# Units 2 to 5 of a gated linear attention: inputs as runs of tokens, transposed by VectorE, with level decays and row products on GpSimd

## The chip, the cores and the metric

The kernel runs on one core of a Trainium2 chip. The metric is device time in microseconds: how long one execution takes, as the median of several.

## The reference

Two blocks follow each other. The first is a gated linear attention over 4 batches, 8 heads, 768 tokens and head size 48. The second is a mixture of four experts whose input is the first one's output, 3072 tokens by 384.

```python
for t in range(S):
    state = alpha[:, :, t, :, None] * state + np.einsum('bhd,bhe->bhde', k[:, :, t], v[:, :, t])
    y[:, :, t] = np.einsum('bhd,bhde->bhe', q[:, :, t], state)
...
p = domain_probs / (domain_probs.sum(-1, keepdims=True) + 1e-09)
for e in range(E):
    h = np.maximum(x @ w1[e], 0.0)
    out += p[:, e:e + 1] * (h @ w2[e])
```

`w1` is 384 x 1024 and `w2` 1024 x 384 for each expert. All inputs and outputs are float32.

## The kernel before

**Units and groups.** A unit is a block of 128 tokens of one batch, all heads: 24 units, numbered in the order in which they are done. Groups of units go through the experts together: units 0 and 1 (group 0), then four groups of four, then units 22 and 23. For each group and expert there is an `up` (eight chunks of 128 hidden columns: `x @ w1` into a PSUM tile `one`, ReLU by ScalarE) and a `down` (`h @ w2` into `ops`, which VectorE adds to the output with the probabilities as a scale, L1079).

**Precision.** Group 0 multiplies plain float32. From group 1 on the weights and activations are split into a high and a low part, and three products are made (`PRODUCTS`, L103; the products with the low part of the activations come last in `down`). VectorE makes the low part of the hidden values in `hidden_rest` (L1009), ahead of `down`. The weights are read from the inputs once, as float32 pieces (`raw`, `load_piece`, L234 for `w1` and L238 for `w2`, four pieces of 384 KB for each matrix and expert), split by ScalarE and VectorE (`split_piece`, L252 and L254), stored to device memory from GpSimd's queue (L255), and read back as pairs later (L225).

**Attention is woven in.** While the experts work on one group, the attention of the next group's units is made beside it. Each unit is a Python generator with about 15 to 20 steps. `deal` (L1099) gives each step a due time from estimated costs, and `advance` (L1155), which is called between expert matmuls, runs the steps that are due. So each engine's queue has a fixed order in which expert and attention instructions alternate, and a waiting instruction holds up everything behind it on its engine. The start is ordered by hand (L1184 to L1196).

**A unit's steps.** Inputs `a` (the decay), `k`, `q` come with tokens in the partitions and have to be transposed to have channels in them (`AT`, `KT`, `QT`; `QT` is multiplied by `AT`). Then come seven levels, each of twice the block size. At a level `li`, ScalarE copies half of QT to a buffer (`copy_q`, L777 or L543), VectorE multiplies half of QT by the decays (`next_q`, L784 or L549) and then multiplies pairs of decays in place to get those of the next level (L786 or L551), and `next_k` does the same for KT (L795 and L796; L560 and L563). TensorE makes scores from these (`sc`, `far`), VectorE merges them by masks into `near` (L813, L616), ScalarE copies them to `lat`, and TensorE multiplies by the values (`yps`) and makes the state's update (`sps`). The diagonal of the scores, a product of q and k summed over channels (`dot`), is made apart.

**Three ways to take the inputs.** `in_runs` (L144) and `in_fours` (L145) say from which unit on a way is used; they are 6 and 10.

- Units 0 to 5: `load` issues one DMA for each of a, k, q (L176; 192 KB, with 192 bytes in a row), and four TensorE transposes each (`turned`, L285) turn them by way of PSUM. ScalarE copies the results to AT (L728) and KT (L737), and VectorE multiplies the third by AT (L756).
- Units 6 to 9: `load` issues four DMAs for each of a, k, q, whose rows are runs of tokens (L171, into `sa`, `sk`, `sq`), and one DMA each for k and q in the old form (L176, into `rk` and `ra`), for `dot`. VectorE transposes blocks of 32 x 32 (`turn`, L723), ScalarE scales AT (L734), VectorE multiplies QT by AT (L754). When the first such unit is loaded, GpSimd clears the run tails once (L165).
- Units 10 to 23 (`in_order`): as before, but q and the decays for `dot` come in rows of four tokens. GpSimd multiplies decays of neighbouring tokens (L510) and q by them (L512); VectorE multiplies the result by k (L522) and sums it (L523), each in two halves.

For units 1 to 9 `own_terms` (L741) makes `dot`: VectorE multiplies q and k (L743), sums the product (L744), and the next unit's k is asked for. This happens in the unit's second step, for unit 1 in its third.

**Queues.** SyncE issues all loads. Its order around the start is: units 0 and 1, four pieces of `w1` of the first expert, unit 2's a, k, q (from `first_unit`), the probabilities (L1189, 48 KB), four pieces of `w2` (at the first `up`, L238), four pieces of `w1` of the second expert, then unit 2's values. `norm_probs` (L267) turns the probabilities by four TensorE transposes (L270) and norms them on VectorE (L272 to L275). Its place is after the first three products of the first `down`. `fill` (L1184) issues matmuls on zeros at the start.

Of the kernel before, what the change touches and what calls it, by code (L numbers as in the profile page):

```python
# [16 lines left out]
AX = mybir.AxisListType  # L17
# [3 lines left out]
def kernel(  # L21
# [11 lines left out]
    nc = tc.nc  # L33

    B, H, S, D = q.shape
    E, DM, F = moe_w1.shape
    P = 128
# [13 lines left out]
    FOUR = 4  # L51
# [3 lines left out]
    n = np.arange(QUAD)[None, :]  # L55
# [4 lines left out]
    t = np.arange(HALF)[None, :]  # L60
# [30 lines left out]
    half = B // 2  # L91
# [13 lines left out]
    row_k = const.tile([P, H, D], F32, name="rk")  # L105
    row_a = const.tile([P, H, FOUR - 1, D], F32, name="ra")
# [34 lines left out]
    HEAD_FIRST = [*(0.06 * j for j in range(1, 8)), 0.5, 0.58, 0.66, 0.74, 0.82, 0.93]  # L141
    HEAD_SECOND = [0.02, 0.06, 0.1, 0.13, 0.16, 0.2, 0.25, 0.31, 0.37, 0.45, 0.52, 0.61, 0.66]
    REST = [0.05, 0.17, 0.3, 0.42, 0.58]
    in_runs = half + B  # L144
    in_fours = half + 2 * B  # L145
    MARGIN = 6.0
    waiting = deque()
# [140 lines left out]
    def first_unit(fill, other):  # L288
# [139 lines left out]
            nc.scalar.copy(out=later_half[:HALF, NP * i:NP * (i + 1)], in_=far[rows[i]])  # L428
        for i in range(1, NQ):
            load_piece(0, i, behind=later_half[:HALF, 0, :1])  # L430
        load(2, "akq")
        take(2, part(second, 0))
        take(3, part(second, QUAD))
        take(-1, part(second, HALF, HALF))
# [55 lines left out]
    def in_order(u):  # L490
        cb, b = units[u]
        k = u - in_fours
# [16 lines left out]
        for j in range(1, FOUR - 1):  # L509
            nc.gpsimd.tensor_mul(row_a[:, :, j], row_a[:, :, j - 1], row_a[:, :, j])  # L510
        for i, t in enumerate(fours[u]):
            nc.gpsimd.tensor_mul(t[:, :, 1:], t[:, :, 1:], row_a[:, H // 2 * i:H // 2 * (i + 1)])  # L512
        yield
        load(u + 1, "a")
        KT = work.tile([P, NP, P], F32, name="KT", bufs=6)
# [3 lines left out]
        dots = hid.tile([P, H, FOUR], F32, name="dot", bufs=1)  # L519
        for i, t in enumerate(fours.pop(u)):  # L520
            some = slice(H // 2 * i, H // 2 * (i + 1))
            nc.vector.tensor_mul(t, t, row_k[:, some].unsqueeze(2).broadcast_to([P, H // 2, FOUR, D]))  # L522
            nc.vector.reduce_sum(out=dots[:, some], in_=t, axis=AX.X)  # L523
            yield
        load(u + 1, "k")
# [19 lines left out]
        def next_q(li):  # L545
            m = LEVELS[li]
            qv = halves(QT, m)[:, :, :, 1, :]
            dv = halved(decs[li])
            nc.vector.tensor_mul(qv, qv, spread(dv[:, :, :, 0], m))  # L549
            dec = dv[:, :, :, 0] if li < 6 else work.tile([P, NP, 1], F32, name="dec6", bufs=9)  # L550
            nc.vector.tensor_mul(dec, dv[:, :, :, 0], dv[:, :, :, 1])  # L551
            decs.append(dec)

        def next_k(li):
# [156 lines left out]
    def attention(u):  # L711
# [26 lines left out]
        dots = hid.tile([P, H, FOUR], F32, name="dot", bufs=1)  # L738
        dot = dots.rearrange("p h f -> p (h f)")[:, :H]

        def own_terms():  # L741
            own = rk[:, :, :D]
            nc.vector.tensor_mul(own, rq[:, :, :D], rk[:, :, :D])  # L743
            nc.vector.reduce_sum(out=dot, in_=own, axis=AX.X)  # L744
            load(after, "k")


        own_late = u == 1
        if not own_late:
            own_terms()  # L750
        yield
        if u >= in_runs:
            turn("q", QT)
# [1 line left out]
        else:  # L755
            nc.vector.tensor_mul(QT, turned(pair(rq)), AT)  # L756
        if own_late:
            own_terms()
        load(after, "q")
        yield  # L760

# [18 lines left out]
        def next_q(li):  # L780
            m = LEVELS[li]
            qv = halves(QT, m)[:, :, :, 1, :]
            dv = halved(decs[li])
            nc.vector.tensor_mul(qv, qv, spread(dv[:, :, :, 0], m))  # L784
            dec = dv[:, :, :, 0] if li < 6 else work.tile([P, NP, 1], F32, name="dec6", bufs=9)
            nc.vector.tensor_mul(dec, dv[:, :, :, 0], dv[:, :, :, 1])  # L786
            decs.append(dec)

        def next_k(li):
# [159 lines left out]
    def up(gi, e, fc, spent, slots=None):  # L949
        n = len(groups[gi]) * P  # L950
        lo, hi = (slots.start * P, slots.stop * P) if slots else (0, n)
        begins, ends = lo == 0, hi == n
        c, f = divmod(fc, FPQ)
        i = first_piece(gi, e) + c
        if fc == 0 and begins:
            for k in range(NQ):
                hidden[k] = hid.tile([P, 2, FPQ, NT], F32 if gi == 0 else F32R, name="hT", bufs=NQ)
        if gi == fc == 0 and begins:
            for k in range(NQ):
                load_piece(1, e * NQ + k, beside=True)  # L960
        beside = BESIDE[(gi, e) == (1, 0)]
        if fresh(gi) and fc in beside:
            making.append(split_piece(1, first_piece(gi, e) + beside[fc]))
        if gi == 0 and e > 0 and fc in SPLIT_AT:
            making.append(split_piece(0, e * NQ + SPLIT_AT[fc]))
        if gi == 0 and begins and e + 1 < E and fc == (FCH - 1 if e == 0 else FCH // 2):
            for k in range(NQ):
                load_piece(0, (e + 1) * NQ + k)
        col = slice(f * P, (f + 1) * P)
        if gi > 0:  # L970
            w = wt[0][i].rearrange("p t (c f) -> p t c f", f=QF)[:, :, :, col]
        else:
            w = wt[0][i].rearrange("p (c f) -> p c f", f=QF)[:, :, col]
        parts = [hidden[c][:, part, f, lo:hi] for part in range(2)]
        one = ps.tile([P, NT], F32, name="one", tag="g", bufs=4)[:, :hi - lo]
        if gi == 0:
            for kc in range(KC):
                nc.tensor.matmul(one, lhsT=w[:, kc], rhs=xTs[gi][:, 0, kc, lo:hi],  # L978
                                 start=(kc == 0), stop=(kc == KC - 1))
            advance(spent)  # L980
            nc.scalar.activation(out=parts[0], in_=one, func=ACT.Relu)
        else:
            turns = [(kc, *parts) for parts in PRODUCTS for kc in range(KC)]
            for k, (kc, of_w, of_x) in enumerate(turns):
                nc.tensor.matmul(one, lhsT=w[:, of_w, kc], rhs=x_part(gi, of_x)[:, kc, :n],  # L985
                                 start=k == 0, stop=k == len(turns) - 1)
            nc.scalar.activation(out=parts[0], in_=one, func=ACT.Relu)  # L987
            while finish:
                hidden_rest(*finish.popleft())
            finish.append((one, parts))  # L990
        while finish and fc == FCH - 1:
            hidden_rest(*finish.popleft())
        background()
        if f == FPQ - 1 and ends:
            if gi == 0:
                if e == E - 1:
                    load_piece(1, i + NQ, held=wt[1][i])
            elif gi != LAST - 1:
                load_piece(0, i + AHEAD, held=wt[0].pop(i))
            while late:  # L1000
                load_piece(1, late.popleft())
            while stores:
                stores.popleft()()
        if gi > 0:
            advance(spent)
# [155 lines left out]
    with tc.manual_schedule():  # L1161
        nc.scalar.dma_start(out=ident_all, in_=nc.inline_tensor(ident_np, name="ident_c").ap())
        nc.scalar.dma_start(out=masks_all, in_=nc.inline_tensor(mask_np, name="masks_c").ap())
        nc.gpsimd.memset(sts[B - 1], 0.0)
        for nm in "akq":
            for r in (early[nm], apart[nm]):
                nc.gpsimd.memset(r[:, :, D:], 0.0)
        nc.gpsimd.memset(lat[HALF:, :, :HALF], 0.0)
        for t in values + blocks:
            nc.gpsimd.memset(t, 0.0)  # L1170
        for t in sts[:-1]:
            nc.gpsimd.memset(t, 0.0)

        load(0, "aqkv")
        load(1, "akqv")

        idle = ps.tile([P, DM], F32, name="idle", tag="g", bufs=4)
        zeros = sts[B - 1].rearrange("p a i d -> p (a i d)")  # L1180

        def fill(times, n=P):
            for _ in range(times):
                nc.tensor.matmul(idle[:, :n], lhsT=zeros[:, :P], rhs=zeros[:, :n], start=True, stop=True)  # L1184

        runs = [None, attention(1)]
        fill(7)
        runs[0] = first_unit(fill, runs[1])
        nc.sync.dma_start(out=p_rows, in_=moe_domain_probs.rearrange("(n p) e -> n p e", p=P))  # L1189

        span = cost(0, 0, 0) * FCH / 2 + cost(1, 0, 0)
        runs.append(norm_probs())
        waiting.extend((span * (k + 1) / 15, u, runs[u]) for k, u in (
            *((k, 1) for k in range(3)), (3, 0), (4, 1), *((k, 1) for k in range(6, 10)),
            (9.5, 2), (10, 1), (10.5, 0), *((k, 1) for k in range(11, 14))))
        for fc in range(FCH):  # L1196
            up(0, 0, fc, cost(0, 0, 0) / 2, slice(0, 1))
        down(0, 0, [0])
        while waiting:
            next(waiting.popleft()[2], None)  # L1200
        clock = 0.0
        waiting.extend((1.0 + k, 1, runs[1]) for k in range(2))
        waiting.extend(deal())

        for gi, e in tasks:
            rest = gi == e == 0
            for fc in range(FCH):
                up(gi, e, fc, cost(0, gi, e) / (2 if rest else 1), slice(1, len(groups[0])) if rest else None)
            each = len(groups[gi]) if gi > 0 else 1
            turns = [range(k, k + each) for k in range(rest, len(groups[gi]), each)]  # L1210
            for slots in turns:
                down(gi, e, slots)
        while stores:
            stores.popleft()()
# [28 lines left out]
```

## Time and profile before

| what | before |
|---|---|
| median of the runs shown | 972.08 us (971.99 to 972.23, 3 runs) |
| the profiled execution's own time | 971.34 us |
| its span, first to last instruction | 969.3 us |
| mean granted TensorE clock | 1.000 |
| data moved by DMAs | 185.26 MB, 191 GB/s over the span |
| VectorE transpose of 128x512 (L723) | 1.08 to 1.18 us, x12 |
| TensorE transposes (L285) | 116 matmuls of 0.27 us, overlapping |
| ScalarE copies of a transposed input (L728, L737) | 0.58 and 0.59 us, x5 each |
| VectorE decays (L786, L551) | 0.13 to 1.3 us, 158 in all, 48 us |
| VectorE row products (L522) and sums (L523) | 0.95 us each, x28 each |
| GpSimd products of rows (L510, L512) | 1.02 and 1.48 us on average, x28 each |

The profile comes from one execution. In its lists PE is TensorE's matmuls, PEld its weight loads, DVE VectorE, ACT ScalarE, POOL GpSimd and SP SyncE; a q behind the name means the engine's sequencer or DMA queue. A timeline row has a start, a duration, the engine, the line, and what is written from what; in brackets is how long the engine sat idle before it and what ended that. In the chain of work that ended last, a row has a start and the time that its part of the chain took. A row of waits has the total, the number and the longest one.

### The profile page before, as it was taken

The page shows a single profiled execution, that of the slowest core. Times are in us where ns is not written, and L with a number is a line of the kernel's source. Part 1 is how long each engine was busy: PE and PEld are TensorE (multiplying, and loading weights), DVE is VectorE, ACT ScalarE, POOL GpSimd, SP SyncE. Part 2 cuts the span into 40 slices and gives each one's busy share as a digit, 9 for nine tenths or more (in the row PEclk, how much of TensorE's full clock was granted, in tenths as well). Part 3 has the DMA queues.
Part 4 walks back from the last instruction along what each step waited for, and adds up shares of the span by engine and source line. Part 5 has one row for each costly group of instructions (what it writes and reads, how often), then busy time and mean ns, then how long its engine had stood idle before and what let it go on. Part 6 is the DMA issues. An engine that isn't in the chain of part 4 may idle for free.

```text
span 969.3 us, 20948 instructions
## 1 busy us (share of the span) xinstructions
PE 957.8 (99%) x8456; PEld 857.2 (88%) x8456; DVE 585.0 (60%) x1164; ACT 384.4 (40%) x838; POOL 126.6 (13%) x173
## 2 busy tenths in 40 slices
PE   8999999999999999999999999999999999999998
PEld 7787778988979989989889899899898899999997
DVE  6677778477787856757747668668776212221222
ACT  5787656454462441441441432434344122021111
POOL 3000110011213212021121120220220000000000
PEclk9999999999999999999999999999999999999999
DMA  8998859395964787865677864679870007060601
GB/s 164 298 292 247 253 143 325 104 358 143 307 217 129 224 288 208 269 202 136 199 252 204 303 217 113 198 211 253 273 233 16 34 1 260 1 260 2 257 20 33
DMA packets 168740, 185.26 MB, mean 191 GB/s; under 512 B 83980, under 2 KB 148364, under 8 KB 168644
## 3 DMA queue, kind: packets, MB, share of 16 engines
q1 hardware_dynamic: 162180, 154.07, 52.7%
q0 software_dynamic: 6016, 29.49, 8.2%
q8 instruction: 67, 1.10, 0.5%
q10 hardware_dynamic: 448, 0.36, 0.1%
q14 instruction: 29, 0.24, 0.1%
HBM read 151.37 MB, written 32.51 MB: 190 GB/s over the span
## 4 chain that ended last, share of the span: by engine, by line
PE 90%; DVE 5%; ACT 3%; issue 1%; DMA 0%; SPq 0%; DVEq 0%; POOL 0%; ACTq 0%; POOLq 0%
PE ops L1053 41%; PE one L985 33%; PE one L978 4%; PE sc L596 3%; PE yps L670 2%; PE sc L803 2%; PE yps L898 1%; PE tp L285 1%; DVE hT L1009 1%; DVE w L254 1%; ACT qb L777 1%; DVE near L813 1%; PE sps L606 0%; PE far L859 0%; PE idle L1184 0%
## 5 line engine op out<-in xcount | busy, mean ns | idle before, releaser
L1053 PE MATMUL ops<-w,hT 128*128 128x384 f32 x2112 | 377.2, 337 | 2.2 <-DVE hT L1009 2.0
L1053 PEld LDWEIGHTS ops<-w,hT 128*128 128x128 f32 x2112 | 365.3, 188 | 7.9 <-DVE hT L1009 3.9
L985 PE MATMUL one<-xT,w 128*128 128x512 f32 x1440 | 333.2, 391 | 0.1
L985 PEld LDWEIGHTS one<-xT,w 128*128 128x128 f32 x1440 | 269.4, 188 | 56.8 <-DVE hT L1009 1.0
L987 ACT ACTIVATE hT<-one 128x512 fp32r<-128x512 f32 (+1 forms) x192 | 108.0, 562 | 315.5 <-PE one L985 314.9
L1009 DVE SCALAR_TENSOR_TENSOR hT<-one,hT 128x512 fp32r<-128x512 f32 (+1 forms) x192 | 121.1, 642 | 103.6 <-ACT hT L987 103.5
L1079 DVE SCALAR_TENSOR_TENSOR acc<-ops,p_all,acc 128x384 f32<-128x384 f32 x66 | 38.8, 611 | 81.9 <-PE ops L1053 81.8
L549 DVE TENSOR_TENSOR QT<-QT,AT 128x256 f32<-128x256 f32 x70 | 32.9, 471 | 49.6 <-ACT qb L543 39.2
L777 ACT COPY qb<-QT 64x256 f32<-64x256 f32 x126 | 51.5, 409 | 21.3 <-DVE QT L784 13.9
L466 POOL TENSOR_TENSOR st<-st,dec 64x192 f32<-64x192 f32 x32 | 18.6, 582 | 277.9 <-PE yps L670 218.5
L978 PE MATMUL one<-xT,raw 128*128 128x256 f32 (+1 forms) x240 | 45.8, 340 | 0.6 <-issue 0.5
L1053 PE MATMUL ops<-raw,hT 128*128 128x384 f32 x128 | 45.4, 493 | 0.7 <-DMA raw<-in_moe_w_dram 0.7
L1088 POOL DMA_DIRECT2D out_dram<-acc x22 | 12.0, 548 | 249.1 <-DVE acc L1079 249.1
L978 PEld LDWEIGHTS one<-xT,raw 128*128 128x128 f32 x240 | 38.1, 191 | 5.4 <-issue 0.6
L510 POOL TENSOR_TENSOR ra<-ra 128x384 f32<-128x384 f32 x28 | 28.5, 1018 | 99.0 <-DMA ra<-in_alpha_dram 97.4
L255 POOL DMA_DIRECT2D kept<-w x32 | 17.5, 547 | 182.9 <-DVE w L254 83.0
L512 POOL TENSOR_TENSOR raw<-raw,ra 128x576 f32<-128x576 f32 x28 | 40.8, 1478 | 1.1
L784 DVE TENSOR_TENSOR QT<-QT,AT 128x256 f32<-128x256 f32 x60 | 26.0, 434 | 23.6 <-ACT qb L777 23.0
L813 DVE COPY_PREDICATED near<-masks,sc 128x256 f32<-128x256 uint8 x54 | 28.8, 534 | 11.8 <-PE sc L803 10.8
L985 PE MATMUL one<-raw,w 128*128 128x256 f32 x288 | 35.2, 283 | 0.0
L543 ACT COPY qb<-QT 64x256 f32<-64x256 f32 x80 | 32.1, 401 | 7.5 <-DVE QT L549 4.0
L985 PEld LDWEIGHTS one<-raw,w 128*128 128x128 f32 x288 | 35.1, 192 | 0.0
(166 smaller groups left out, 960.8 us busy)
## 6 DMA issues: line engine op xcount, KB each, us to landing
w<-kept SPq DMA_DIRECT2D x108, 768.0 KB, 6.6
kept<-w POOLq DMA_DIRECT2D x32, 768.0 KB, 6.0
raw<-in_moe_w_dram SPq DMA_DIRECT2D x44, 384.0 KB, 7.4
raw<-in_q_dram SPq DMA_DIRECT2D x112, 96.0 KB, 3.0
rv<-in_v_dram SPq DMA_DIRECT2D x24, 192.0 KB, 3.3
out_dram<-acc POOLq DMA_DIRECT2D x22, 192.0 KB, 2.5
rk<-in_k_dram SPq DMA_DIRECT2D x18, 192.0 KB, 3.1
sa<-in_alpha_dram SPq DMA_DIRECT2D x36, 88.0 KB, 3.7
```

The lines of the kernel that those rows point to most:

```text
L512: nc.gpsimd.tensor_mul(t[:, :, 1:], t[:, :, 1:], row_a[:, H // 2 * i:H // 2 * (i + 1)])
L543: nc.scalar.copy(out=qbs[li][rows, :, i, :].rearrange("p a (b r) -> p a b r", r=m), in_=qv[rows])
L549: nc.vector.tensor_mul(qv, qv, spread(dv[:, :, :, 0], m))
L596: nc.tensor.matmul(banks[li // 2 - 1][HALF * s:HALF * (s + 1), li % 2, 2 * p:2 * p + 2, :], lhsT=KTs[li][:, p, HALF * s:HALF * (s + 1)], r ...
L777: nc.scalar.copy(out=qb[rows, :, i, :].rearrange("p a (b r) -> p a b r", r=m), in_=qv[rows])
L813: nc.vector.copy_predicated(near.rearrange("p a (b two r) -> p a b two r", two=2, r=m)[:, :, :, 1, :], mk.unsqueeze(1).broadcast_to([P, H, ...
L978: nc.tensor.matmul(one, lhsT=w[:, kc], rhs=xTs[gi][:, 0, kc, lo:hi], start=(kc == 0), stop=(kc == KC - 1))
L985: nc.tensor.matmul(one, lhsT=w[:, of_w, kc], rhs=x_part(gi, of_x)[:, kc, :n], start=k == 0, stop=k == len(turns) - 1)
L987: nc.scalar.activation(out=parts[0], in_=one, func=ACT.Relu)
L1009: nc.vector.scalar_tensor_tensor(out=low, in0=x, scalar=0.0, in1=top.bitcast(F32), op0=ALU.max, op1=ALU.subtract)
L1053: nc.tensor.matmul(sums[slot], lhsT=h, rhs=w, start=(n == begins[slot]), stop=(n == ends[slot]))
L1079: nc.vector.scalar_tensor_tensor(out=acc, in0=part, scalar=scale, in1=acc, op0=ALU.mult, op1=ALU.add)
```

## The change

Four things are changed. `in_runs` becomes 2, so that units 2 to 5 are loaded and turned as units 6 to 9 are. Unit 2's loads and the load of the probabilities move to the first `up`, behind the four pieces of `w2`. The multiplication of decays at each level goes to GpSimd, for all units but the first. GpSimd also multiplies by k in `in_order` (L522 before, then at L513), and makes the product of q and k for units 2 to 9 in the second step; the sum of it (L744 before, L753 after) and the load of the next unit's k move to the third step, behind QT.

```diff
-    in_runs = half + B
+    in_runs = half
...
         for i in range(1, NQ):
             load_piece(0, i, behind=later_half[:HALF, 0, :1])
-        load(2, "akq")
         take(2, part(second, 0))
...
         for i, t in enumerate(fours[u]):
-            nc.gpsimd.tensor_mul(t[:, :, 1:], t[:, :, 1:], row_a[:, H // 2 * i:H // 2 * (i + 1)])
+            some = slice(H // 2 * i, H // 2 * (i + 1))
+            nc.gpsimd.tensor_mul(t[:, :, 1:], t[:, :, 1:], row_a[:, some])
+            nc.gpsimd.tensor_mul(t, t, row_k[:, some].unsqueeze(2).broadcast_to([P, H // 2, FOUR, D]))
         yield
...
             some = slice(H // 2 * i, H // 2 * (i + 1))
-            nc.vector.tensor_mul(t, t, row_k[:, some].unsqueeze(2).broadcast_to([P, H // 2, FOUR, D]))
             nc.vector.reduce_sum(out=dots[:, some], in_=t, axis=AX.X)
...
-            nc.vector.tensor_mul(dec, dv[:, :, :, 0], dv[:, :, :, 1])
+            nc.gpsimd.tensor_mul(dec, dv[:, :, :, 0], dv[:, :, :, 1])
             decs.append(dec)
...
-        def own_terms():
-            own = rk[:, :, :D]
-            nc.vector.tensor_mul(own, rq[:, :, :D], rk[:, :, :D])
-            nc.vector.reduce_sum(out=dot, in_=own, axis=AX.X)
-            load(after, "k")
...
+        own = rk[:, :, :D]
         own_late = u == 1
         if not own_late:
-            own_terms()
+            nc.gpsimd.tensor_mul(own, rq[:, :, :D], own)
         yield
...
         if own_late:
-            own_terms()
+            nc.vector.tensor_mul(own, rq[:, :, :D], own)
+        nc.vector.reduce_sum(out=dot, in_=own, axis=AX.X)
+        load(after, "k")
         load(after, "q")
         yield
...
         if gi == fc == 0 and begins:
             for k in range(NQ):
                 load_piece(1, e * NQ + k, beside=True)
+            if e == 0:
+                load(2, "akq")
+                nc.sync.dma_start(out=p_rows, in_=moe_domain_probs.rearrange("(n p) e -> n p e", p=P))
...
         runs[0] = first_unit(fill, runs[1])
-        nc.sync.dma_start(out=p_rows, in_=moe_domain_probs.rearrange("(n p) e -> n p e", p=P))
```

The line of the decays is changed in both `in_order` (L551) and `attention` (L786 before, L782 after).

More of the change, by code (lines that the diff above doesn't have):

```diff
@@ L785, in next_q @@
             dec = dv[:, :, :, 0] if li < 6 else work.tile([P, NP, 1], F32, name="dec6", bufs=9)
-            nc.vector.tensor_mul(dec, dv[:, :, :, 0], dv[:, :, :, 1])
+            nc.gpsimd.tensor_mul(dec, dv[:, :, :, 0], dv[:, :, :, 1])
             decs.append(dec)
```

## The prediction

> **What bounds the kernel now.** I read the page's first part first, then the chain, then TensorE's waits, and last the two places on which the change acts: the start (SyncE's and TensorE's timelines) and VectorE beside GpSimd.
>
> The page, busy time and the chain by engine:
>
> ```profile
> PE 957.8 (99%) x8456; PEld 857.2 (88%) x8456; DVE 585.0 (60%) x1164; ACT 384.4 (40%) x838; POOL 126.6 (13%) x173
> ...
> PE 90%; DVE 5%; ACT 3%; issue 1%; DMA 0%; SPq 0%; DVEq 0%; POOL 0%; ACTq 0%; POOLq 0%
> ```
>
> TensorE is the bound: 90% of the chain is its own work. A gain has to be matmuls taken away or one of its few waits; relief of VectorE by itself is worth next to nothing. Parts of the chain and of TensorE's waits:
>
> ```profile
> 40.95 0.59 PE tp L285 x4
> ...
> 42.21 0.44 PE tp L285 x4
> ...
> 99.59 0.91 issue
> 100.50 0.63 PE tp L285 x4
> ```
>
> ```profile
> PE ops L1053 <- DVE hT L1009: 2.0, 3, 1.1
> ...
> PE tp L285 <- issue: 0.9, 1, 0.9
> ```
>
> The reader is to see that a group of four transposes of units 2 to 5 stands on the chain with 0.44 us or a little more, and that TensorE waits hardly anywhere: 2.0 us for VectorE's low parts (L1009, at 203, 243 and 284 us), 0.9 us ahead of a transpose.
>
> **Part 1, transposes leave TensorE.** Units 2 to 5 have three groups of four (a, k, q): 12 groups. The chain shows most at 0.44 and single ones at 0.59, 0.63 and 0.66 (with a wait of 0.07 inside): about 5.3 + 0.5 = 5.8 us of TensorE's own time, all on the path. The 0.91 us of "issue" goes with the group at 100.50. Together -6.7 us.
>
> In their place come 12 VectorE transposes (L723, 1.08 to 1.18 us each: 13 us), beside matmuls. What is late next: unit 2's first score products, at 52.84, come 1.5 us sooner on TensorE, while their chain through VectorE and ScalarE gets slower (three transposes of 1.1 us in a row where there were copies of 0.58 us; then two levels whose decay of 0.43 us becomes GpSimd's 0.73 us plus two handovers). Between 66 and 78 us the chain runs through ScalarE already, so there is little slack. I take +1.0 us for such waits over the four units; bounds 0 (slack covers all) and +4 (about 1 us a unit).
>
> **Part 2, the start.** SyncE's queue, and TensorE beside it:
>
> ```profile
> 15.66 1.43 SPq L234 DMA_DIRECT2D raw<-in_moe_w_dram  x3
> 17.18 0.44 SPq L176 DMA_DIRECT2D sa<-in_alpha_dram  x1
> 17.72 0.60 SPq L176 DMA_DIRECT2D sk<-in_k_dram  x1
> 18.42 3.20 SPq L176 DMA_DIRECT2D sq<-in_q_dram  x1
> 21.67 0.81 SPq L1189 DMA_DIRECT2D w<-in_moe_domain_probs_dram  x1
> 22.53 3.83 SPq L238 DMA_DIRECT2D raw<-in_moe_w_dram  x4
> ```
>
> ```profile
> 27.51 2.20 PE L1053 MATMUL ops<-raw,hT 128*128 128x384 f32 x6 [0.73 <-DMA raw<-in_moe_w_dram]
> 29.64 0.65 PE L270 MATMUL tp<-ident,w 24*128 24x24 f32 x4
> 30.46 0.66 PE L859 MATMUL far<-qb,KT 128*64 128x128 f32 x8 [0.16 <-ACT qb L777]
> ```
>
> After the change the four pieces of the second weight come first, then unit 2's loads, now 14 instead of 3, and only then the probabilities (L1189), which four TensorE transposes (L270) need. Their place in TensorE's order is the same: behind three of the first down products, ahead of `far`. So L270 waits, and behind it stand all of TensorE's later work and VectorE's L272. When does the table land? Before, 2.2 MB (three pieces of 0.39, three inputs of 0.20, the table, a piece) were asked for from 15.66 on, and L1053 shows the last of them in at 27.5; with some 2 us until data flow that is 225 GB/s, while the page's second slice has 298. After, three and four pieces, three run tensors of 344 KB (two DMAs of 88 KB and two of 80 each) and two of 196 KB stand ahead of the table: 4.2 MB, hence landing at 31.8 (298 GB/s) to 36.5 us (225). Long rows fill most of it, so I take 33.5. The weight being early, L1053 starts without its 0.73 us, and TensorE stands before L270 from 28.9 on: a stall of 4.6 us. L270 starts 3.9 us later than 29.64; the 0.16 us ahead of `far` goes. **+3.7 us**, bounds +2.0 and +6.9. The first weights of the next expert, asked for still later, are used at 50.25 only: nothing. The three fills of run tails (L165, 0.15 us) move to this place on an idle GpSimd: nothing.
>
> **Part 3, more DMAs.** Units 3 to 5 too have 14 issues where 3 were (0.43 us each when nothing holds them: +4.7 us of SyncE a unit), and k's now wait for VectorE's sum (L744) and stand ahead of weights. Second-weight pieces of expert 2, issued from 83.13 on, are used at 98.30; some 6 us later and 6 to 7 us to land still just meets that. I take +0.3 us, bounds 0 and +2.
>
> **Part 4, decays and row products on GpSimd.** Off VectorE go 158 decays (L786 and L551, 48 us in all), 28 row products (L522, 26.5 us) and eight own products of 0.55 (L743; unit 1's stays). GpSimd's row products give its price: 384 elements 1.01 us, 576 1.44, so 2.2 ns an element and 0.16 us; a row product of 768 takes 1.9 us, a unit's seven decays 2.3 us. Its 127 us grow by about 110, far below the span. Does the exchange cost? Two things speak for it. VectorE now waits for a decay before the next level's QT product, and for both row products before L523; low parts (L1009) are queued behind, and TensorE waits for those. And the two engines get in each other's way:
>
> ```profile
> 318.51 3.02 POOL L512 TENSOR_TENSOR raw<-raw,ra 128x576 f32<-128x576 f32 x2
> ...
> 318.88 1.36 DVE L549 TENSOR_TENSOR QT<-QT,AT 128x256 f32<-128x256 f32 x1 [1.32 <-ACT qb L543]
> ...
> 320.27 1.31 DVE L551 TENSOR_TENSOR AT<-AT 128x16 f32<-128x16 f32 x1
> ```
>
> Two VectorE products of usually 0.43 and 0.19 us end when GpSimd's end, while L1009, which reads one operand from PSUM, keeps its 0.68 us beside GpSimd. The Trainium skill says the same (SBUF — State Buffer, section "SBUF: two separate sides"): a VectorE operation with two SBUF inputs and a GpSimd operation that reads SBUF take a port in turn, the first for the whole instruction. By that rule moving a product to a slower engine can make VectorE later than keeping it; here that is the rival below.
>
> I work the steady state out on one unit (395 to 411 us). GpSimd ends unit u's last decay at about 395 and then needs 2 x 1.1 + 2 x 1.44 + 2 x 1.9 = 8.9 us for the rows, with a locked-out VectorE product in between up to 405.3. VectorE reaches the second sum at 404.8 instead of 405.2 and waits about 0.6; QT's product then starts 0.1 to 0.2 us later than now. The low parts at 398.37 and 399.29 slip by about 0.7, and TensorE needs them 4.2 to 7.7 us after 398.45 (its down products come with the high parts first: 24 products at 0.176 us before the first low part of a pair). So nothing from 340 us on. In group 1 (142 to 300 us) VectorE is full (17.75 of 20 us at 260 to 280) and TensorE waits 2.35 us for it, at 203.13 (0.67), 243.49, 280.20, 282.64 (0.23), 284.18 (1.13) and 323.94. Ahead of 203 VectorE loses 0.55 (L743) and 0.43 (L786), ahead of 284 two row products and three decays, about 2.9 us. I take -1.3 of the 2.35; bounds -2.35 and +4.
>
> **Sum.** -5.8 - 0.9 + 1.0 + 3.7 + 0.3 - 1.3 = -3.0 us. The profiled execution took 971.34 us (span 969.3 and 2.0 around it), which gives 968.3; the median of the runs shown is 0.74 above it, so 972.08 - 3.0 = **969.1 us**. A measurement of this kernel tells about 0.2% (1.9 us) from no change.
>
> **Rivals.**
>
> 1. *The start takes back what the transposes give.* The table lands at the late bound (+3.2 over my value), or TensorE restarts slowly. For the second: the first 4.7 us of matmuls (1.21 to 5.9) run 0.42 us each, spaced 0.21, against 0.27 and 0.11 later, so a slow start costs half of its length, 2.3 us. Against it: no idle time of TensorE over 1.2 us stands in this trace. The result would be 971.4 to 972.3. Chance 0.24. The Trainium skill (TensorE: Matmul & The Clock Gate, section "Why this matters for your kernels") warns of idle gaps over about 3 us between matmuls; no gap here is long enough to show it, and by that rule the stall of 4.6 us could bring the slow start.
>
> 2. *Slower: GpSimd holds VectorE back.* In each of 14 units 8.9 us of row work, and in group 1 the decays behind it, make a low part later than the 4.2 us that TensorE gives it after the first of its `ops`. From there each further 0.5 us is 7 us over the units; also in group 1 alone a unit's wait of 2 us would do: 976. For it: the locked pair above and VectorE's load before 340 us. Against it: 3.5 us of slack in the unit worked out. Chance 0.22.
>
> 3. *Hidden anyway.* The chain of units 2 to 5 over VectorE and ScalarE, not TensorE, sets their products, and part 1 gives 3 us less (its bound): 972.1. For it: ScalarE on the chain from 66 to 78 us. Chance 0.06.
>
> My forecast holds 0.48 and, for reasons of size alone, ends below 970.1; some of the first rival does too (0.04). **Faster 0.52, within 0.2% 0.26, slower 0.22.** The range goes from 965.5 (start at its low bound, all of VectorE's waits gone) to 976 (the second rival).
>
> **What would show it.** Right: no L285 of units 2 to 5 in TensorE's rows; one TensorE wait of 3 to 6 us ahead of L270 at about 29 us; at 140 us a lead of 2 to 4 us over before; at 285 us a little more; the same pace from 340 on. Wrong: L270 without a wait (then I lose 3.7 us of cost), waits of `ops` for L1009 beyond 2 us in all, VectorE idle ahead of L523 or QT's products with GpSimd named, or waits of L803 and L859 adding up beyond 2 us.

## The result and the profile after

| | before | after |
|---|---|---|
| median | 972.04 us (971.67 to 972.75, 13 runs) | 974.02 us (971.90 to 975.60, 13 runs) |
| ratio, 95% interval | | 1.0020 (1.0012 to 1.0029) |
| the profiled execution: time, span | 971.34, 969.3 us | 975.60, 973.7 us |
| mean granted TensorE clock | 1.000 | 0.995 |
| HBM read | 151.37 MB | 154.71 MB |

The kernel became 2.0 us slower; 3.0 us faster was forecast, and the result lies inside the range. The profiled execution of after is the slowest of its 13, so the terms read from its trace add up to 2.7 us more (+4.7) than the medians differ.

The page of after, busy time and the chain by engine:

```profile
PE 954.9 (98%) x8408; PEld 855.0 (88%) x8408; DVE 532.8 (55%) x982; ACT 382.5 (39%) x834; POOL 257.3 (26%) x367
...
PE 91%; DMA 3%; DVE 3%; issue 1%; ACT 1%; SPq 0%; DVEq 0%; POOL 0%; ACTq 0%
```

The 48 transposes are gone from TensorE (8456 to 8408), VectorE is down by 52 us, GpSimd up by 131, and a DMA share of 3% has come into the chain. TensorE's waits in after (total, number, longest):

```profile
PE tp L270 <- DMA w<-in_moe_domain_probs_dram: 5.9, 1, 5.9
PE sps L472 <- ACT AT L911: 1.9, 2, 1.3
PE sc L799 <- issue: 1.5, 1, 1.5
...
PE sc L799 <- ACT qb L773: 1.1, 1, 1.1
PE ops L1052 <- DVE hT L1008: 0.7, 1, 0.7
PE far L855 <- ACT qb L773: 0.6, 1, 0.6
```

The first row is the stall for the probabilities. The rows for ScalarE's `AT` and `qb` are four new waits, 3.6 us together, at 78 to 121 us, where units 2 to 5 are made. (The 1.5 us of "issue" lie at 27 to 28.6 us, ahead of the stall, which would only have been longer without them.) The 2.0 us for low parts have become 0.7.

To see where the time went I compared the start of each expert matmul (the n-th `one` or `ops`, 4208 in both kernels). The lag of after:

| stretch, by before's time | lag at its end | what it adds | forecast |
|---|---|---|---|
| start, to the 60th product (34.4 us) | +9.5 us | +9.5 | +3.7 |
| units 2 to 5, to the 320th (123.5 us) | +7.7 | -1.8 | -5.4 |
| group 1, to the 1200th (343 us) | +4.7 | -3.0 | -1.3 |
| the rest | +4.7 | 0 | 0 |

SyncE's queue and TensorE in after at the start:

```profile
17.43 3.45 SPq L238 DMA_DIRECT2D raw<-in_moe_w_dram  x4
20.98 2.81 SPq L171 DMA_DIRECT2D sa<-in_alpha_dram  x4
24.58 5.48 SPq L171 DMA_DIRECT2D sk<-in_k_dram  x4
30.11 0.43 SPq L176 DMA_DIRECT2D rk<-in_k_dram  x1
30.65 1.94 SPq L171 DMA_DIRECT2D sq<-in_q_dram  x4
32.63 0.43 SPq L176 DMA_DIRECT2D ra<-in_q_dram  x1
33.10 0.58 SPq L959 DMA_DIRECT2D w<-in_moe_domain_probs_dram  x1
```

```profile
36.95 0.67 PE L270 MATMUL tp<-ident,w 24*128 24x24 f32 x4 [5.87 <-DMA w<-in_moe_domain_probs_dram]
37.55 1.12 PE L855 MATMUL far<-qb,KT 128*64 128x128 f32 x8
38.45 1.92 PE L799 MATMUL sc<-qb,KT 128*64 128x64 f32 x32
```

The issues themselves are held: four of `sk` take 5.48 us, where the four of `sq` behind them take 1.94, and the fourth goes out at 29.75, just after the last weight piece landed at 29.73. SyncE's waits from 20 to 31 us name the cause:

```profile
SPq L171 <- DMA raw<-in_moe_w_dram: 4.8, 4, 2.2
```

Four of unit 2's issues wait 4.8 us in all for weight pieces to land, though they write other tiles. The semaphores in the trace tell why: the program marks SyncE's loads here with eight semaphores taken in turn, so a load is issued only when the eighth before it has landed, and `sk`'s four stand eighth behind the four pieces of `w2`. So the table is asked for at 33.10, 11.4 us later than before, and TensorE gets it at 36.95. Then `far` takes 1.12 us for its 0.66 of before and `sc` 1.92 for 1.10. The granted clock in stretches of 4 us (columns: busy times, PEclk, DMA share, GB/s):

```profile
35.00:39.00 4.00, 2.05 (x24) 2.01 (x26) 1.00 (x4) 0.28 (x1) 0.00 (x0) 0.64 0.93 279
39.00:43.00 4.00, 4.00 (x61) 2.69 (x60) 1.36 (x4) 2.89 (x6) 0.00 (x0) 0.51 0.40 140
43.00:47.00 4.00, 4.00 (x43) 2.46 (x43) 2.68 (x5) 2.03 (x4) 1.25 (x2) 1.00 0.52 147
```

Half speed until about 43 us, then full again. Of the 9.5 us, 7.3 are L270's later start (36.95 against 29.64) and 2.2 the slow products behind it (net of 0.2 us of small waits that before has there).

### The profile page after: what moved, and what is told of

Read it like the earlier page. It is cut to its first block, busy times and chain, and to the rows that moved or that the text cites. A ratio compares the mean times of both kernels' runs of the same rounds, so it can differ in the third digit from the quotient of the medians.

```text
span 973.7 us, 21014 instructions
## 1 busy us (share of the span) xinstructions
PE 954.9 (98%) x8408; PEld 855.0 (88%) x8408; DVE 532.8 (55%) x982; ACT 382.5 (39%) x834; POOL 257.3 (26%) x367
## 3 DMA queue, kind: packets, MB, share of 16 engines
HBM read 154.71 MB, written 32.51 MB: 192 GB/s over the span
## 4 chain that ended last, share of the span: by engine, by line
PE 91%; DMA 3%; DVE 3%; issue 1%; ACT 1%; SPq 0%; DVEq 0%; POOL 0%; ACTq 0%
PE ops L1052 40%; PE one L984 36%; PE one L977 3%; PE sc L596 3%; PE yps L670 2%; PE sc L799 2%; DMA raw<-in_moe_w_dram 2%; PE yps L894 1%; PE tp L285 1%; DVE w L254 1%; DMA sk<-in_k_dram 1%; ACT qb L773 0%; PE sps L606 0%; PE far L855 0%; DMA sq<-in_q_dram 0%
## 5 line engine op out<-in xcount | busy, mean ns | idle before, releaser
L1078 DVE SCALAR_TENSOR_TENSOR acc<-ops,p_all,acc 128x384 f32<-128x384 f32 x66 | 38.8, 610 | 88.0 <-PE ops L1052 87.8
L551 POOL TENSOR_TENSOR AT<-AT 128x256 f32<-128x256 f32 (+5 forms) x60 | 28.0, 467 | 189.0 <-DVE QT L549 188.9
L549 DVE TENSOR_TENSOR QT<-QT,AT 128x256 f32<-128x256 f32 x70 | 33.8, 483 | 63.1 <-ACT qb L543 46.9
L773 ACT COPY qb<-QT 64x256 f32<-64x256 f32 x126 | 51.5, 409 | 24.0 <-DVE QT L780 12.7
L513 POOL TENSOR_TENSOR raw<-raw,rk 128x768 f32<-128x768 f32 x28 | 53.2, 1899 | 2.2
L782 POOL TENSOR_TENSOR AT<-AT 128x256 f32<-128x256 f32 (+5 forms) x54 | 24.7, 457 | 94.0 <-DVE QT L780 93.8
L512 POOL TENSOR_TENSOR raw<-raw,ra 128x576 f32<-128x576 f32 x28 | 45.1, 1611 | 1.1
L780 DVE TENSOR_TENSOR QT<-QT,AT 128x256 f32<-128x256 f32 x60 | 27.5, 459 | 31.2 <-ACT qb L773 30.1
L1052 PEld LDWEIGHTS ops<-raw,hT 128*128 128x128 f32 x128 | 23.7, 193 | 14.1 <-ACT hT L980 0.2
```

The lines of the kernel that those rows point to most:

```text
L512: nc.gpsimd.tensor_mul(t[:, :, 1:], t[:, :, 1:], row_a[:, some])
L513: nc.gpsimd.tensor_mul(t, t, row_k[:, some].unsqueeze(2).broadcast_to([P, H // 2, FOUR, D]))
L551: nc.gpsimd.tensor_mul(dec, dv[:, :, :, 0], dv[:, :, :, 1])
L773: nc.scalar.copy(out=qb[rows, :, i, :].rearrange("p a (b r) -> p a b r", r=m), in_=qv[rows])
L1052: nc.tensor.matmul(sums[slot], lhsT=h, rhs=w, start=(n == begins[slot]), stop=(n == ends[slot]))
L1078: nc.vector.scalar_tensor_tensor(out=acc, in0=part, scalar=scale, in1=acc, op0=ALU.mult, op1=ALU.add)
```

## The experiments

Medians stand with the ratio to before and its interval; "lag" is that of the expert matmuls against before, in the profiled execution.

### The start

**probs_early**: after, with the table's load back ahead of the first `up`.

```diff
                 load(2, "akq")
-                nc.sync.dma_start(out=p_rows, in_=moe_domain_probs...)
...
         runs[0] = first_unit(fill, runs[1])
+        nc.sync.dma_start(out=p_rows, in_=moe_domain_probs...)
```

> The changed kernel with one line put back: the probabilities are asked for right after the first unit's code, ahead of the second weight, as before the change; unit 2's loads stay behind the weights. Theory (the table's landing sets the start): L270 no longer waits 5.9 us, the granted clock stays at 1.00 from 30 to 60 us, the 55th matmul of the experts comes within 1 us of its time before the change (8.3 us late now), and all of it is kept to the end: about 966 us. Rival (the start is bound by the 14 loads or by unit 1's attention, and the table is only the first to show it): another wait of 3 us or more stands in the place, and the time stays at 970 to 972.

969.60 us, 0.9972 (0.9963 to 0.9982). L270 waits no more, the clock is 1.00 until the last products, the lag at the 60th product is +0.4. The forecast of 966 is missed all the same. By medians the place of this one load costs 4.4 us and turns the sign of the change. It is less than the 9.1 us by which the 60th product moves: at the 320th the lag is already +1.7, because units 2 to 5 now wait more (below). What TensorE lost at the start had hidden part of those waits: the stretch from the 60th to the 320th product takes 90.4 us here and 87.3 in after, with 6.2 and 3.6 us of waits in it.

**table_first**: after, with the same load ahead of unit 2's loads, still behind the four weight pieces.

```diff
+                nc.sync.dma_start(out=p_rows, in_=moe_domain_probs...)
                 load(2, "akq")
-                nc.sync.dma_start(out=p_rows, in_=moe_domain_probs...)
```

> The changed kernel, with the load of the probabilities ahead of unit 2's 14 loads, still behind the four weight pieces. If the 14 loads make the table late: TensorE's wait at L270 falls from 5.9 us to 1 us or less, no slow clock follows, and the time is about 8 us less at the 60th matmul of the experts and 970 to 971 at the end. If the weight pieces ahead make it late: the wait stays over 3 us and the time over 972.

969.90 us, 0.9978 (0.9966 to 0.9990), no wait at L270: the table is asked for at 20.09. So unit 2's 14 loads make it late; the weight pieces alone don't. The profiled execution (971.47 us) loses time further on: a piece of second weight comes 2.70 us late at 64 us, and 3.41 us at half clock follow.

**before_late**: before, with unit 2's three loads and the table at the change's place.

```diff
-        load(2, "akq")
...
                 load_piece(1, e * NQ + k, beside=True)
+            if e == 0:
+                load(2, "akq")
+                nc.sync.dma_start(out=p_rows, in_=moe_domain_probs...)
...
-        nc.sync.dma_start(out=p_rows, in_=moe_domain_probs...)
```

> The kernel before with one part of the change alone: unit 2's loads (three, in the old form) and then the probabilities move behind the second weight. Theory (what stands ahead of the table decides): the queue ahead of it is 0.9 MB and 11 issues shorter than in the changed kernel, so L270 waits 1 to 3 us instead of 5.9, short of what slows the clock, and the time is 973 to 974.5. Rival (the place alone makes the whole loss): a wait of 5 us or more and 977 or above. Other rival: no wait, 972.

972.18 us, 1.0002 (0.9994 to 1.0011). L270 waits 1.38 us, and the lag is +0.8: with three loads the place is almost free. The clock stays 1.00. The table is asked for at 27.44 and there at 30.65, 3.2 us later; in after it takes 3.9 (33.10 to 36.95). So what differs between the two is mostly when the table is asked for.

**The slow clock** (warm, warm24, warm32): after, with n matmuls on constants ahead of L270, n = 60, 24 and 32.

```diff
+        for _ in range(n):
+            nc.tensor.matmul(tp..., lhsT=ident, rhs=ident[:, :E * NBLK], start=True, stop=True)
```

> The changed kernel with 60 matmuls on constants, 96 columns each, put ahead of L270 on TensorE; they write the tile that L270 overwrites, and nothing else is changed. They keep TensorE busy for about 5 of the 5.9 us of its wait. Theory (the idle gap slows the clock and the slow clock costs some 2.4 us after the wait): granted clock 1.00 from 30 to 60 us, L270 at the same time (36.9), the products behind it at full speed, 971 to 972. Rival (the clock has no part in it): same pace behind the wait, 974.

> The changed kernel with 24 matmuls of 96 columns on constants put into TensorE's queue ahead of L270, some 5 us of them at 0.21 us each, so that they end before the table lands. If the idle gap slows the products behind it: between the 48th and the 60th expert matmul 1 to 2.3 us less than in the changed kernel beyond the wait, and 972 to 973 at the end. If the gap costs its own length only: no difference, 974.

> The changed kernel with 32 matmuls of 96 columns on constants ahead of L270, 0.23 us each, 7.3 us in all, so that they end when the table lands (about 37.2 us). With 24 of them 1.97 us stayed idle and the products behind L270 were as slow as without any (far 1.12 us, sc 1.92 us). If the slow clock behind an idle gap is a cost of its own: far 0.66 and sc 1.10 us, granted clock 1.00 between 35 and 43 us, and 1.8 to 2.2 us less than the changed kernel from the 60th expert matmul on, 972 us at the end. If not: the 60th matmul as late as before, 974.

979.84 us, 1.0075 (1.0062 to 1.0088) with 60: they last 13.5 us, far past the landing of the table (median of six executions, one of which took 2474.88 us; the others 978.5 to 980.1). 974.16, 1.0019 (1.0009 to 1.0030) with 24: they end 1.97 us before it, and `far` and `sc` are as slow as without, but the clock is halved for 3.4 us instead of 6.8. 974.34, 1.0027 (1.0016 to 1.0037) with 32, which end when it lands. TensorE's timeline of warm32 (the profile has two rows for each of these matmuls):

```profile
29.91 7.28 PE L270 MATMUL tp<-ident 128*128 128x96 f32 x64
37.12 0.66 PE L272 MATMUL tp<-ident,w 24*128 24x24 f32 x4
37.70 0.66 PE L857 MATMUL far<-qb,KT 128*64 128x128 f32 x8
38.19 1.10 PE L801 MATMUL sc<-qb,KT 128*64 128x64 f32 x32
```

Nothing idle, clock 1.00, normal durations, and the 60th product 2.25 us earlier than in after (lag +7.24 for +9.49). From L270's start to the 60th product it is 4.5 us in warm32, 5.7 in warm24 and 6.9 in after. In the rows the slow clock is thus shown with its price: 1.3 us for the 3.4 us at half clock in warm24, 2.4 for the 6.0 us that TensorE works at half clock in after. The medians of warm32 and after don't show it (974.34 and 974.02, overlapping intervals). The added matmuls hold TensorE to 37.1 us also in executions in which the table may land earlier, and after's profiled execution is its slowest; which of these hides the gain isn't settled.

### Units 2 to 5

**runs_only**: before, with `in_runs = half` alone.

> The kernel before with one edit: units 2 to 5 are loaded as runs and transposed by VectorE; decays, row products, the place of unit 2's loads and of the probabilities stay as before. Theory A (the transposes leave TensorE, and the waits of units 2 to 5 give back only 1 us, as predicted): 972.1 - 5.7 = about 966.5 us. Theory B (those waits give it all back, whatever GpSimd does): TensorE's waits between 60 and 125 us add up to 5 to 7 us in this kernel too, lead at 142 us between -1 and +1 us, time 971 to 973. Theory C (the waits need GpSimd's decays beside the runs): waits under 2 us, 967 to 968.

981.75 us, 1.0103 (1.0089 to 1.0116). Unit 2's 14 loads at their old place hold up the second weight: the first down product waits 4.65 us for `raw` and restarts at half speed (4.21 us for six products, 2.20 in before); the lag is +6.6 at the 60th. From there to the 320th it grows by 3.6 more, though the transposes are gone: `yps`, `sps` and `sc` wait 6.1 us for ScalarE, and two of these waits (1.38 and 1.35 us, close together) are followed by another 3.4 us at half clock, from 101.5 us on. The waits fit theory B; the time doesn't, for a start that no theory had. GpSimd's decays are not needed for these waits.

**early_six**: probs_early with `in_runs = half + B`, so TensorE transposes again and units 2 to 5 have three loads each.

> probs_early with in_runs at 6 again: units 2 to 5 are transposed by TensorE from one DMA each, and what is left of the change is GpSimd's part (decays, row products, products of q and k for units 2 to 9) and unit 2's loads behind the weights. Theory (the new TensorE waits at 78, 99, 109 and 121 us come with the runs and VectorE's transposes, and the gain between 142 and 345 us is GpSimd's): none of these four waits, 3 us gained from 142 to 345, and 969 us. Rival (these waits come from decays on GpSimd): 3 us of waits between 70 and 125 us, 971 to 972.

968.14 us, 0.9960 (0.9948 to 0.9971). No wait over 0.5 us between 60 and 125 us. The runs in units 2 to 5, meant to take 5.8 us off TensorE, make the kernel slower by 1.5 us (969.60 with them).

**dma_kept**: probs_early, where units 2 to 5 still issue their 14 loads (and one more, for `a`), but TensorE transposes plain copies.

```diff
-            if u >= in_runs and nm == "a":
+            if u >= half + B and nm == "a":
...
-        if u >= in_runs:
+        if u >= half + B:
             turn("a", AT)
```

(likewise for k and q, with plain tiles of their own)

> The changed kernel with the probabilities asked for early. Units 2 to 5 still issue all 14 loads (the run tensors, read by nobody for these units) and one more for a in its plain form (15), but TensorE transposes them again. Theory 'transfers' (the 14 issues and 5 MB more delay weights and inputs): waits between 60 and 125 us stay at about 6 us, and the transposes' 5.8 us come on top: 974 to 976. Theory 'chain' (VectorE's three transposes in a row make scores late): waits go, and the time falls to that of the kernel that keeps TensorE's transposes and the old loads, about 968 to 969.

974.45 us (970.39 to 976.99), 1.0023 (1.0011 to 1.0034). TensorE now waits for the loads directly: 1.7 us for `ra`, 1.9 for ScalarE's copy behind it. The median fits "transfers", but the executions spread over 6.6 us, and the profiled one (971.76 us) stands 2.7 below the median: its waits explain the median in part only.

**no_loads**: probs_early without the loads of a, k and q for units 3 to 5.

```diff
         for nm in names:
+            if 2 < u < 6 and nm != "v":
+                continue
```

> The changed kernel with the probabilities asked for early, and without the loads of a, k and q for units 3 to 5: these units compute on unit 2's inputs, so part of the computation is left out; every instruction of the engines stays. Theory 'transfers' (the 14 loads of a unit, 1.42 MB where 0.59 MB were, fill the queue and hold up weights and inputs): the waits of TensorE between 65 and 115 us (6 us in all) fall under 2 us, and the time to 964 to 966. Theory 'chain' (VectorE's three transposes in a row, then the levels, are late whatever lands when): the waits stay at 5 to 6 us and the time at 969 to 970.

966.81 us, 0.9943 (0.9930 to 0.9955): between the two theories. TensorE's waits from 60 to 125 us, first probs_early, then no_loads:

```profile
PE far L855 <- ACT qb L773: 1.8, 2, 1.2
PE sps L472 <- ACT AT L911: 1.3, 1, 1.3
PE ops L1051 <- DMA raw<-in_moe_w_dram: 1.2, 1, 1.2
PE sc L799 <- ACT qb L773: 1.1, 1, 1.1
PE yps L894 <- ACT lat L872: 0.8, 1, 0.8
```

```profile
PE sps L474 <- ACT AT L913: 1.7, 2, 1.1
PE sc L801 <- ACT qb L775: 1.1, 1, 1.1
PE far L857 <- ACT qb L775: 0.6, 1, 0.6
```

And the stretch from 80 to 100 us, likewise (PE, PEld, DVE, ACT, POOL, PEclk, DMA share, GB/s):

```profile
80.00:100.00 20.00, 16.72 (x222) 14.13 (x222) 15.79 (x29) 14.72 (x36) 5.00 (x10) 1.00 0.98 288
```

```profile
80.00:100.00 20.00, 18.31 (x225) 14.74 (x224) 15.80 (x32) 14.94 (x37) 5.94 (x12) 1.00 0.54 195
```

With the loads the DMA engines are full (0.98), and a weight and several inputs are late; without, they are half idle. At the 320th product the two differ by 3.5 us (+1.68 and -1.85), which is the transfers' part (2.8 by medians; an upper one, since before's 0.59 MB a unit are gone too). The four waits that are left, 3.4 us, are the chain's part, and they are the same four, at the same places, as in after. From the 60th to the 320th product no_loads takes 87.1 us, after 87.3: behind the stall at the start, the loads of units 3 to 5 cost after next to nothing.

**five_old**: six_old (below) with runs for unit 5 alone.

```diff
-    in_runs = half + B
+    in_runs = half + B - 1
```

> The kernel before with the GpSimd part, and runs for unit 5 alone (three groups of transposes leave TensorE, 1.4 us). Theory 'transfers': unit 5's loads fall at 85 to 105 us, where the mean busy share of the DMA engines is 0.9, and 0.8 MB more of them costs some 3 us of transfer, partly seen: 967 to 969 against 968.05 without. Theory 'hidden': 968.05 - 1.4 = 966.7.

968.04 us, 0.9958 (0.9945 to 0.9970), the same as six_old's 968.05. Even one unit's runs pay nothing: from the 60th to the 320th product TensorE loses 1.3 us of transposes and gains 0.9 of waits, above all one of the four, the 1.07 us of `sc` for ScalarE's `qb` (at 112.6 us), and `sc` stands 0.4 us longer; 0.1 us is left. The profiled execution lags by 0.7 us at the 60th product already, ahead of any difference between the two kernels.

### GpSimd's part

**early_decays_v**: probs_early, with the level decays back on VectorE.

```diff
-            nc.gpsimd.tensor_mul(dec, dv[:, :, :, 0], dv[:, :, :, 1])
+            nc.vector.tensor_mul(dec, dv[:, :, :, 0], dv[:, :, :, 1])
```

> The changed kernel with the probabilities asked for early, and the level decays back on VectorE; row products and own products stay on GpSimd. If the handovers to GpSimd make the waits of units 2 to 5, the lag of 1.7 us at 142 us against the kernel before turns to a lead of 2 us or more; if the runs make them, it stays at 1 to 2 us. If the decays make the gain between 142 and 345 us (3 us), it goes, and the time is about 972 to 973; if the row products and own products make it, it stays, and the time is 969 to 970.

975.12 us, 1.0031 (1.0020 to 1.0042), against 969.60 with the decays on GpSimd. The waits of units 2 to 5 remain (5.0 us from 60 to 125 us, 6.2 in probs_early). Up to the 1000th product (297 us) the row products and the products of q and k alone still gain 2.05 us from the 320th on, where probs_early gains 2.6. Then the lag jumps by 4.2 us between 297 and 343 us. VectorE and GpSimd there:

```profile
319.21 1.72 DVE L551 TENSOR_TENSOR AT<-AT 128x16 f32<-128x16 f32 x1
320.85 0.41 DVE L563 TENSOR_TENSOR KT<-KT,AT 128x256 f32<-128x256 f32 x1
321.19 0.68 DVE L1007 SCALAR_TENSOR_TENSOR hT<-one,hT 128x512 fp32r<-128x512 f32 x1
321.79 1.04 DVE L549 TENSOR_TENSOR QT<-QT,AT 128x256 f32<-128x256 f32 x1
322.86 1.68 DVE L551 TENSOR_TENSOR AT<-AT 128x8 f32<-128x8 f32 x1
324.46 0.41 DVE L563 TENSOR_TENSOR KT<-KT,AT 128x256 f32<-128x256 f32 x1
324.79 0.68 DVE L1007 SCALAR_TENSOR_TENSOR hT<-one,hT 128x512 fp32r<-128x512 f32 x1
```

```profile
318.97 1.91 POOL L513 TENSOR_TENSOR raw<-raw,rk 128x768 f32<-128x768 f32 x1
320.85 1.69 POOL L512 TENSOR_TENSOR raw<-raw,ra 128x576 f32<-128x576 f32 x1
322.62 1.89 POOL L513 TENSOR_TENSOR raw<-raw,rk 128x768 f32<-128x768 f32 x1
```

Decays of 16 and 8 columns take 1.72 and 1.68 us instead of about 0.2 and end when GpSimd's row products end; the low part (L1007) is queued behind, and TensorE waits 2.23 us for it at 323.30; 3.4 us at half clock follow. This is the second rival's mechanism. In after it doesn't reach TensorE at this place: decays and row products share GpSimd's queue, so the rows start only behind the last decay (at 320.8 us in probs_early, 314.9 here), when VectorE's levels are done. It isn't gone either: 17 VectorE products in after last over 0.3 us more than the median of their kind, by 11.4 us in all, against 21 and 13.6 us in before and 29 and 32.7 us here. Without the decays GpSimd's part is a loss, mostly by this one collision; the decays moved with them keep the gain more than they make it. The Trainium skill (SBUF — State Buffer, section "SBUF: two separate sides") has the lock that these rows show.

**six_old**: before, with the GpSimd part alone.

> The kernel before with the GpSimd part alone: decays, row products and own products on GpSimd, TensorE's transposes, unit 2's loads and the probabilities at their old places. If the gain is GpSimd's alone, the time is 968 us or a little less (968.14 with unit 2's loads behind the second weight, which showed +0.4 us until 160 us); if the place of unit 2's loads helped, 969 or more. No wait of TensorE over 1.2 us anywhere after 20 us.

968.05 us, 0.9963 (0.9950 to 0.9976). The lag goes from -0.35 at the 320th to -3.36 at the 1200th product and stays: the same -3.0 as in after. 1.66 us of it are TensorE waits that the profile shows (2.36 us between 145 and 345 us in before, 0.70 here); the rest is in no wait of the matmuls, but `ops` and `one` stand 0.8 and 0.6 us shorter in sum, and TensorE's weight loads waited 3.9 us for low parts ahead of `ops` in before, 1.3 in after. With early_six and five_old this is the fastest of all that leave nothing out: 3.9 us less than before, 6.0 less than after.

## Why the prediction was wrong, point by point

- **Part 2, the start (+3.7; bounds +2.0 to +6.9)** is the step that failed: +9.5 us in the profiled execution. It took the table's landing, 33.5, from the bytes ahead of it (4.2 MB at 225 to 298 GB/s), and put SyncE's issues at nothing. The table was asked for at 33.10 only, with 4.8 us of waits for weight pieces in the queue ahead of it, and was there at 36.95, later than the late bound of 36.5 (which as a cost is +6.7, not +6.9, with the 0.16 us ahead of `far` taken off as in the middle value); the page's slice of 298 GB/s was the wrong row to lean to. table_first and probs_early show that it is the 14 loads, before_late that their bytes are not all of it: its table has 0.8 MB less ahead, 3.7 us at 225 GB/s, and is there 6.3 us sooner. The row of `sq` with 3.20 us for one issue, quoted from before's queue, is no sign of this hold: there SyncE waits 2.9 us for TensorE's `one` (L978).
- **Slow restart** stood in the first rival as an alternative to the late landing, and not in the sum. Both came, and one caused the other: 2.4 us. Its price, 2.3 us, was right by luck: it was half of 4.7 us, while TensorE worked 6.0 us at half clock and lost 0.4 of that time. The rival's mechanism is what happened at the start; with its +3.2 and +2.3 added together instead of chosen from, the forecast would have been 974.6. That is near the median, but in part because the errors of parts 1 and 4 have opposite signs.
- **Part 1, -6.7 and +1.0 for waits of the chain**: 5.4 us of transposes left TensorE, not 5.8, and the 0.9 us of "issue" went. The waits were mis-sized: 3.6 us in after, inside the bounds 0 to +4, at `sps`, `sc` and `far` as the closing part named them ("waits of L803 and L859 adding up beyond 2 us"; `sps` was not named). Another 0.9 us is in no wait: `sc`, `yps` and `one` stand longer in sum. The third rival, "part 1 gives 3 us less", had this, with too small a chance. The chain ahead of the longest of these waits (87.8 to 99.2 us) runs through VectorE's three transposes of 1.1 us, ScalarE's copies and two weight splits (L254); which of them is the one to move was not tried.
- **Part 3, more DMAs, +0.3 (0 to +2)**: in after about 0.2 us, the difference to no_loads over the same stretch (-1.8 and -2.0). But that is so only because TensorE stands still at the start; without that stall it is up to 3.5 us (no_loads against probs_early), beyond the bound. A second-weight piece is late there, as supposed, but already at 65.5 us (1.2 us in probs_early), earlier than the place that I had worked out.
- **Part 4, -1.3 in group 1 (bounds -2.35 to +4)**: -3.0. Direction and place were right, steady state nothing as worked out. The size was low: all but 0.7 us of the low parts' waits went, and 1.3 us more that stand in no wait of the matmuls. What the decays and the row products each give was taken apart from one side only (early_decays_v). GpSimd's price was right for the row product (1.9 us forecast, 1.899 measured) and low for the rest: a unit's seven decays take 3.0 us, not 2.3, and GpSimd's busy time grew by 131 us, not 110. VectorE's long products became no more than in before (17 against 21), so the second rival's lock cost nothing more, for the reason that early_decays_v shows.

Sum in the profiled execution: +9.5 - 1.8 - 3.0 = +4.7 us where -3.0 was forecast; 5.8 of the 7.7 between are the start.

## What to carry to other kernels

Price a moved load by the whole queue that it is moved behind, issue by issue, with what each issue waits for, and at the rate that this stage shows, not the best slice; then look at who stands in order behind its reader. Taking work off the bounding engine gains nothing if the replacement brings more transfers into a stage whose DMA engines are already 0.73 to 0.93 busy and lengthens the chain that feeds that engine. When long products move to an engine that shares a port, see whether the short ones can move with them, so that one queue puts the long ones behind the short ones; here that was seen at one place.

## What the runs showed of the hardware

- The length of an idle gap of TensorE alone doesn't tell whether the clock is halved. It was after gaps of 1.97 us (warm24), 2.23 (early_decays_v), 2.70 (table_first), 4.65 (runs_only) and 5.87 (after), but not after 1.88 (dma_kept), and it was after 1.38 and 1.35 us close together (runs_only; PEclk 0.50 from 101.5 us on). From dma_kept, then from runs_only:

```profile
82.47 0.63 PE L287 MATMUL tp<-ident,ra 128*128 128x128 f32 x4 [1.88 <-ACT AT L730]
```

```profile
98.96 1.08 PE L898 MATMUL yps<-lat,rv 128*32 128x128 f32 x32 [1.38 <-ACT lat L876]
101.39 0.83 PE L473 MATMUL sps<-rv,AT 128*32 128x48 f32 x32 [1.35 <-ACT AT L915]
```

In the traces' record of the clock each stretch between two changes lasts a multiple of 3.41 us (3.41 or 6.83 slow; 30.72 or 320.85 full). Cut into cells of 3.41 us from the first change on, the 15 traces show half clock behind the cells in which TensorE was idle for 1.93 (warm24), 2.12 and 2.23 (runs_only), 2.13 (early_decays_v), 2.48 (table_first) and 3.41 us (after), and behind none, while the products run at full clock, with 1.71 us (early_decays_v) or less. The Trainium skill (TensorE: Matmul & The Clock Gate, section "Why this matters for your kernels") warns of gaps over about 3 us; the traces disagree on the length, since 1.97 and 2.70 us did it here.

- Kernels with the 14 loads in units 2 to 5 and no stall ahead of them spread more: 967.1 to 971.1 us (probs_early) and 970.4 to 977.0 (dma_kept), against 967.7 to 968.7 (six_old). In probs_early the two longest executions, 971.04 and 971.10 us, are those with the lowest mean clock (0.997 and 0.998).
